# An adaLN transformer block on one core: the work re-cut into items whose issue order on every engine is fixed in the kernel, with four MLP chunks of 512 tokens

## The chip, the cores and the metric

The kernel runs on one core of one Trainium2 chip. The time is device microseconds of one execution, and lower is better. All inputs and the output are bf16 in device memory (HBM). The page of the profile calls the engines PE (TensorE, matmuls; PEld is its weight load), DVE (VectorE), ACT (ScalarE), POOL (GpSimd) and SP (SyncE, which here only starts DMAs).

## What is computed

2048 tokens of width 448 pass through two halves of a block. Each half is modulated by vectors made from a condition `c`. Cut to what matters:

```python
mod = silu(c) @ w_mod                      # six vectors sa, ca, ga, sb, cb, gb of 448
h = layernorm(x) * (1 + ca) + sa
q, k, v = h @ wqkv                         # 16 heads of 28
# position s sees s, s-2, s-4, ... s-14 (window 8, dilation 2; masked below 0)
x = x + ga * (softmax(q k^T * 28**-0.5 over the 8) v) @ wo
h = layernorm(x) * (1 + cb) + sb
y = layernorm(h)
x = x + gb * (gelu(y @ w1 + b1) @ w2 + b2) # 448 -> 1792 -> 448
```

Even and odd positions never see each other, so the kernel loads the even tokens as blocks 0 to 7 and the odd ones as blocks 8 to 15, and the dilated window becomes 8 neighbouring columns.

## The kernel before, in words

**Start.** SP loads `c`, the first four token blocks and the weights needed first; eleven dummy matmuls (`idle_ps`, L144) run meanwhile. `ps_col` (L236) gives the columns `ca` and `sa`. The weights of q and k are copied into a layout padded to 32 per head (`Wqk`, L249 to L254).

**Front end**, once for each four blocks (512 tokens): statistics and normalise on DVE (`ln_params`, L163, with a power on POOL at L173; `normalize`, L176), 16 transposes on PE into `ptr` (L194), four DVE passes that scale and shift into `hT` (L198), then eight `pq` groups of four 512-column matmuls (L206). ACT moves the four q tiles out of PSUM (L210), DVE the four k tiles (L212).

**Attention**, 17 blocks `g` of 121 queries against 128 keys (`attention_block`, L323): `pv` (L330, moved out by ACT), the logits `lt` in two halves of eight 28-row matmuls each (L341; each half alternates between two of the four 32-row strips of the array), exp on ACT (L347), a multiply by a banded mask on DVE (L351), `po` (16 small matmuls, L363), a division on DVE (L365, L367), four transposes `pt` (L371), moved into `oT` by ACT (L377). `wo_block` (L381) multiplies by `wo` (already scaled by `ga`) and DVE adds the residual (L387) into a tile of its own, `x1_all`.

**MLP**, 8 steps `j` of 256 tokens: `mlp_front` (L391) runs two layer norms in a row for each block on DVE (L395 on POOL prepares the residual plus bias), a DMA transpose into `yT` (L407), then 14 weight tiles in groups of four: `p1` (L418, 256 columns a matmul) and one gelu a group (L422, 1024 columns). `mlp_back` (L446) multiplies by `w2` (L451), and `mlp_finish` (L437) adds the residual on DVE (L440) and stores four blocks at a time. The last step runs its second matmul fused into the first (`w2_partial`, L431 and L434).

**Order.** Exp and gelu need different tables on ACT, and a switch is an ACT_TABLE_LOAD. So the kernel runs five phases (L456): some attention blocks, then one or two MLP steps, and `order_after` (L58) adds scheduling edges that keep the exps of a phase together and the gelus together. `mlp_back` of a phase is put among the attention blocks of the next. Within these edges the tile framework's scheduler interleaves the instructions of each engine. PSUM has eight banks: `ps_lt` two tiles of two banks (shared by `ptr`, `lt`, `p1`), `ps_a` two (`po`, `pt`, `pw`), `ps_b` two (`pq`, `pv`, the modulation rows, `p2`). `w2_scale_piece` (L313) multiplies `w2` by `gb` in 14 pieces in the first phase.

Of the kernel before, what the change touches and what calls it, by code (L numbers as in the profile page):

```python
# [14 lines left out]
DP = 512  # L15
# [13 lines left out]
NIDLE = 11  # L29
SCHED = mybir.DependencyInfo(mybir.DependencyClass.NoSync, mybir.DependencyReason.SCHED_ONLY)  # L30
SYNC = mybir.DependencyInfo(mybir.DependencyClass.Sync, mybir.DependencyReason.SCHED_ONLY)


@with_exitstack
def kernel(
# [31 lines left out]

    bulk_dmas = []
# [8 lines left out]
    ps_a = ctx.enter_context(tc.tile_pool(name="ps_a", bufs=2, space=bass.MemoryType.PSUM))  # L77
    ps_b = ctx.enter_context(tc.tile_pool(name="ps_b", bufs=2, space=bass.MemoryType.PSUM))

    def ps_att(shape, dtype, name):  # L80
        return ps_a.tile(shape, dtype, name=name, tag="a1")

    def ps_small(shape, dtype, name):
        return ps_b.tile(shape, dtype, name=name, tag="b1")
# [5 lines left out]
    x1_all = cst.tile([128, NBLK, D], BF16, name="x1_all")  # L90
    x_all = cst.tile([128, NBLK, D], BF16, name="x_all")
    NX1P = 6
# [3 lines left out]
    def x1_blk(b):  # L96
        return x1_all[:, b, :]
# [10 lines left out]
    ident = cst.tile([128, 128], BF16, name="ident")  # L108
    mask_rest = cst.tile([128, H, BK], BF16, name="mask_rest")
# [8 lines left out]
    wk = ctx.enter_context(tc.tile_pool(name="wk", bufs=3))  # L118
# [3 lines left out]
    stp = stp_cm.__enter__()  # L122
    c_row = stp.tile([1, D], BF16, name="c_row")
    nc.sync.dma_start(out=c_row[:], in_=c)
    xv = xs.rearrange("s (jb p) d -> p s jb d", p=128)
    nc.sync.dma_start(out=x_all[:, 0:4, :], in_=xv[:, 0, 0:4, :])
# [6 lines left out]
    bulk_dmas.append(nc.sync.dma_start(out=x_all[:, 4:8, :], in_=xv[:, 0, 4:8, :]))  # L133

    for zb in zbufs:
        nc.vector.memset(zb[:, D:DP], 0.0)
# [5 lines left out]
    for i in range(NIDLE):  # L142
        idle_ps = ps_att([128, 512], FP32, "idle_ps")
        nc.tensor.matmul(idle_ps[:], lhsT=idle_in[:, 0:128], rhs=idle_in[:], start=True, stop=True)  # L144
# [6 lines left out]
    nc.gpsimd.memset(wmod[64:128, KT - 1, :], 0.0)  # L151
    nc.gpsimd.memset(Wv[64:128, KT - 1, :], 0.0)
    nc.gpsimd.memset(Wqk[64:128, KT - 1, :, :], 0.0)
    for kt in range(KT):
        kr = 128 if kt < KT - 1 else 64
        nc.gpsimd.memset(Wqk[0:kr, kt, :, :].rearrange("p m (r e) -> p m r e", e=32)[:, :, :, DH:32], 0.0)
    pad_ranges = [(0, PADF), (PADF + S, WT)]
# [4 lines left out]

    def ln_params(srcs, nm):  # L163
        n = len(srcs)
        mv = sm.tile([128, n, 2], FP32, name=f"mv_{nm}", tag=f"mv{n}")
        for i, src in enumerate(srcs):
            st = sm.tile([128, 6], FP32, name=f"st_{nm}", tag="st")
            nc.vector.bn_stats(out=st[:], in_=src)  # L168
            nc.vector.bn_aggr(out=mv[:, i, :], in_=st[:])
        tv = sm.tile([128, n], FP32, name=f"tv_{nm}", tag=f"tv{n}")  # L170
        nc.vector.tensor_scalar_add(out=tv[:], in0=mv[:, :, 1], scalar1=EPS)  # L171
        rs = sm.tile([128, n], FP32, name=f"rs_{nm}", tag=f"rs{n}")
        nc.gpsimd.tensor_tensor(out=rs[:], in0=tv[:], in1=neg_half[:, 0:n], op=ALU.pow)  # L173
        return mv, rs

    def normalize(dst, src, mv, rs, i):  # L176
        nc.vector.tensor_scalar(out=dst, in0=src, scalar1=mv[:, i, 0:1], scalar2=rs[:, i:i + 1],  # L177
                                op0=ALU.subtract, op1=ALU.mult)

    zcount = [0]  # L180
# [3 lines left out]

    def front_end_ln(c4):
        bs4 = [c4 * 4 + i for i in range(4)]
        mv, rs = ln_params([x_all[:, b, :] for b in bs4], "ln1")
        ptr = ps_lt.tile([128, KT, 512], BF16, name="ptr", tag="lt")
        for i in range(4):
            z = zbufs[zcount[0] % NZB]  # L190
            zcount[0] += 1
            normalize(z[:, 0:D], x_all[:, bs4[i], :], mv, rs, i)
            for kt in range(KT):
                nc.tensor.transpose(out=ptr[:, kt, i * 128:(i + 1) * 128], in_=z[:, kt * 128:(kt + 1) * 128],  # L194
                                    identity=ident[:])
        c0 = tok_col(bs4[0])
        for kt in range(KT):
            nc.vector.tensor_scalar(out=hT[:, kt, c0:c0 + 512], in0=ptr[:, kt, :], scalar1=ca1_col[:, kt:kt + 1],  # L198
                                    scalar2=sa_col[:, kt:kt + 1], op0=ALU.mult, op1=ALU.add)

    def front_end_qk(c4):
        cc0 = tok_col(c4 * 4)
        for m in range(8):
            pq = ps_small([128, 512], FP32, "pq")
            for kt in range(KT):
                nc.tensor.matmul(pq[:], lhsT=Wqk[:, kt, m, :], rhs=hT[:, kt, cc0:cc0 + 512],  # L206
                                 start=(kt == 0), stop=(kt == KT - 1))
            dst = (qT if m < 4 else kT)[:, m % 4, cc0:cc0 + 512]
            if m < 4:
                nc.scalar.copy(out=dst, in_=pq[:])  # L210
            else:
                nc.vector.tensor_copy(out=dst, in_=pq[:])  # L212
# [14 lines left out]
    silu_bf = stp.tile([128, KT], BF16, name="silu_bf")  # L227
    nc.vector.tensor_tensor(out=silu_bf[:], in0=e_c[:], in1=c_col[:], op=ALU.mult)
    nc.vector.tensor_copy(out=silu_bc[:], in_=silu_bf[:].unsqueeze(2).to_broadcast([128, KT, 128]))

    ps_col = ps_small([128, 2 * KT], FP32, "ps_col")
    for v in range(2):
        for j in range(KT):
            nj = 128 if j < KT - 1 else 64
            for kt in range(KT):
                nc.tensor.matmul(ps_col[0:nj, v * KT + j:v * KT + j + 1],  # L236
                                 lhsT=wmod[:, kt, v * D + j * 128:v * D + j * 128 + nj],
                                 rhs=silu_bf[:, kt:kt + 1], start=(kt == 0), stop=(kt == KT - 1))
# [7 lines left out]
    nc.vector.tensor_copy(out=sa_col[0:64, KT - 1:KT], in_=ps_col[0:64, KT - 1:KT])  # L246
    for kt in range(KT):
        kr = 128 if kt < KT - 1 else 64
        wq_out = Wqk[0:kr, kt, :, :].rearrange("p m (r e) -> p m r e", e=32)[:, :, :, 0:DH]  # L249
        wq_in = wqk_st[0:kr, kt, :].rearrange("p (m r d) -> p m r d", m=8, r=4)  # L250
        if kt in (0, 2):
            nc.vector.tensor_copy(out=wq_out, in_=wq_in)
        else:
            nc.scalar.copy(out=wq_out, in_=wq_in)  # L254

    front_end_ln(0)
    front_end_qk(0)

    stp_cm.__exit__(None, None, None)
    stp_cm = tc.tile_pool(name="setup2", bufs=1)  # L260
    stp = stp_cm.__enter__()
    wmod2 = stp.tile([128, KT, 4 * D], BF16, name="wmod2")
    nc.gpsimd.memset(wmod2[64:128, KT - 1, :], 0.0)
    bulk_dmas += load_ktiles(nc.sync, wmod2, w_mod[:, 2 * D:6 * D], 0)
    nc.gpsimd.memset(wo_s[0:ZR_N, KT - 1, :], 0.0)
    bulk_dmas += load_ktiles(nc.sync, wo_s, A_wo, ZR_N)
    bulk_dmas.append(nc.sync.dma_start(out=x_all[:, 8:NBLK, :], in_=xv[:, 1, :, :]))
    mk0 = nc.gpsimd.memset(mask_rest[:], 1.0)
    wait_for([mk0], wv_loads[1:], "mask building (GpSimd) after the DVE-critical start")
    nc.gpsimd.affine_select(out=mask_rest[:], in_=mask_rest[:], pattern=[[0, H], [1, BK]], compare_op=ALU.is_ge,  # L270
                            fill=0.0, base=WIN - 1, channel_multiplier=-1)
    nc.gpsimd.affine_select(out=mask_rest[:], in_=mask_rest[:], pattern=[[0, H], [-1, BK]], compare_op=ALU.is_ge,
                            fill=0.0, base=0, channel_multiplier=1)
# [5 lines left out]

    def mod_bc(idx, name):  # L280
        pb = ps_small([128, D], FP32, name)
        for kt in range(KT):
            nc.tensor.matmul(pb[:], lhsT=silu_bc[:, kt, :], rhs=wmod2[:, kt, (idx - 2) * D:(idx - 1) * D],
                             start=(kt == 0), stop=(kt == KT - 1))
        return pb

    pb_ga = mod_bc(2, "pb_ga")
    nc.vector.tensor_tensor(out=wo_s[:, 0:KT - 1, :], in0=wo_s[:, 0:KT - 1, :],
                            in1=pb_ga[:, :].unsqueeze(1).to_broadcast([128, KT - 1, D]), op=ALU.mult)
    nc.vector.tensor_tensor(out=wo_s[ZR_N:128, KT - 1, :], in0=wo_s[ZR_N:128, KT - 1, :], in1=pb_ga[ZR_N:128, :],  # L290
                            op=ALU.mult)
# [4 lines left out]
    b2_bc = stp.tile([128, D], BF16, name="b2_bc")  # L296
    bulk_dmas.append(nc.sync.dma_start(out=b2_bc[:], in_=B_b2.partition_broadcast(128)))
    wait_for(bulk_dmas, wv_loads[1:], "bulk loads after the critical loads")
    order_after(bulk_dmas[1:], bulk_dmas[:1], "bulk loads in need-order")
    pb_sb = mod_bc(3, "pb_sb")  # L300
    nc.scalar.copy(out=sb_bc[:], in_=pb_sb[:])
    pb_cb = mod_bc(4, "pb_cb")
    nc.vector.tensor_scalar_add(out=g2_bc[:], in0=pb_cb[:], scalar1=1.0)
# [9 lines left out]
    def w2_scale_piece(n):  # L313
        for _ in range(n):
            if not w2_scale_todo:
                return
# [217 lines left out]
```

## Time and profile before

| what | value |
|---|---|
| median of 3 runs | 227.32 us (226.48 to 229.45) |
| the profiled execution | 226.5 us, span of the core 224.4 us |
| instructions in the span | 4134 |
| busy: PE, PE weight load | 196.3 us (87%), 118.0 us (53%) |
| busy: DVE, ACT, POOL | 149.2 us (66%), 103.1 us (46%), 54.9 us (24%) |
| mean granted PE clock | 0.973 |
| first `pq` matmul starts | 14.52 us |
| first `p1` matmul starts | 77.20 us |
| last PE work ends | about 219.6 us |

The span runs from the first to the last recorded instruction; the execution's time is 2.1 us more. "Busy" of PE is the union of the matmuls' records, each of which lasts from its start until its last column has left the array, so neighbours overlap: a 448-column matmul has a record of 353 ns, while a dense row of them starts one every 0.19 us. To price PE work one therefore takes start to start. The same holds for DVE and ACT to a smaller degree.

### The profile page before, as it was taken

To read this page: it belongs to the slowest core of one execution; us is meant where nothing else is said; L and a number is where in the kernel's file an instruction comes from. 1 tells how busy PE (TensorE), PEld (TensorE's weight loads), DVE (VectorE), ACT (ScalarE), POOL (GpSimd) and SP (SyncE) were. 2 spreads that over 40 slices of the span, in tenths; PEclk is the share of its full clock that TensorE was granted. 3 is DMA by queue.
4 is the path that set the end of the run, shared out by engine and by line. 5 is a ranking of instruction groups with operands and counts; after the bars stand their busy time and mean duration, and the time that the engine had idled before them with its cause. 6 is when DMAs were issued, how large, how long until landed. Compare 5 with 4: busy or idle time off the path is not lost.

```text
span 224.4 us, 4134 instructions
## 1 busy us (share of the span) xinstructions
PE 196.3 (87%) x1671; PEld 118.0 (53%) x1671; DVE 149.2 (66%) x367; ACT 103.1 (46%) x133; POOL 54.9 (24%) x89
## 2 busy tenths in 40 slices
PE   7479985999789899979699988796999899989992
PEld 2343352545364485447585444475854476575760
DVE  2786999999888962587865586858755862561102
ACT  2304376143713068497448316763483257352320
POOL 7399001102214220115340023023213230020000
PEclk9999999999958999999999999889999999999998
DMA  5799960000001111001102201100122011021002
GB/s 186 253 325 319 339 218 0 3 0 0 3 0 23 26 26 25 3 0 26 23 0 50 82 0 26 23 3 1 23 50 82 0 26 23 3 82 23 3 0 82
DMA packets 17766, 13.37 MB, mean 60 GB/s; under 512 B 9042, under 2 KB 16851, under 8 KB 17748
## 3 DMA queue, kind: packets, MB, share of 16 engines
q1 hardware_dynamic: 17748, 13.12, 19.6%
q8 instruction: 13, 0.21, 0.4%
q14 instruction: 5, 0.04, 0.1%
HBM read 9.18 MB, written 1.84 MB: 49 GB/s over the span
## 4 chain that ended last, share of the span: by engine, by line
PE 60%; DVE 21%; ACT 10%; POOL 5%; issue 2%; DVEq 0%; POOLq 0%; ACTq 0%
PE p L418 16%; PE p L451 14%; PE pq L206 9%; PE pw L385 5%; ACT hm L422 4%; DVE et L351 3%; POOL rs_ln L173 3%; PE po L363 3%; DVE st_ln L168 3%; DVE x_all L387 3%; DVE kT L212 2%; PE p L434 2%; PE idle_ps L144 2%; PE pt L371 2%; POOL x1p_ring L395 2%
## 5 line engine op out<-in xcount | busy, mean ns | idle before, releaser
L418 PE MATMUL p<-yT,w_s 128*128 128x256 bf16 x448 | 54.5, 277 | 1.5 <-ACT hm L422 0.7
L418 PEld LDWEIGHTS <-w_s 128*128 128x128 bf16 x448 | 43.6, 99 | 10.1 <-issue 2.9
L173 POOL TENSOR_TENSOR rs_ln<-tv_ln,neg_half 128x1 f32<-128x1 f32 (+1 forms) x36 | 22.5, 628 | 79.8 <-DVE tv_ln L171 76.1
L422 ACT ACTIVATE hm<-p 128x1024 bf16<-128x1024 f32 (+1 forms) x32 | 28.6, 916 | 28.7 <-PE p L418 28.5
L451 PE MATMUL p<-w_s,hm 128*128 128x448 bf16 x196 | 40.1, 353 | 0.0
L347 ACT ACTIVATE et<-lt 128x1024 bf16<-128x1024 f32 x34 | 33.6, 1031 | 8.7 <-PE lt L341 8.6
L206 PE MATMUL pq<-hT,Wqk 128*128 128x512 bf16 x128 | 33.6, 401 | 4.4 <-ACT qT L210 2.7
L395 POOL TENSOR_TENSOR x1p_ring<-x_all,gbb_bc 128x448 f32<-128x448 bf16 x16 | 17.8, 1113 | 65.6 <-DVE x_all L387 60.3
L440 DVE TENSOR_TENSOR x_all<-p,x1p_ring 128x448 bf16<-128x448 f32 x16 | 9.8, 619 | 26.9 <-PE p L451 16.5
L377 ACT COPY oT<-pt 128x484 bf16<-128x484 bf16 (+3 forms) x18 | 9.7, 542 | 36.3 <-PE pt L371 36.3
L451 PEld LDWEIGHTS <-hm 128*128 128x128 bf16 x196 | 18.1, 97 | 15.6
L206 PEld LDWEIGHTS <-Wqk 128*128 128x128 bf16 x128 | 12.7, 102 | 19.7 <-issue 9.2
L168 DVE BATCH_NORM_STATS2 st_ln<-x_all 128x6 f32<-128x448 bf16 x32 | 19.1, 609 | 3.5 <-DMA x_all<-in_A_x_dram 3.3
L351 DVE TENSOR_TENSOR et<-et,mask_rest 128x2048 bf16<-128x2048 bf16 x17 | 20.6, 1209 | 0.0
L330 PE MATMUL pv<-Wv,hT 128*128 128x448 bf16 x68 | 17.2, 354 | 0.2 <-DVE kT L212 0.2
L387 DVE TENSOR_TENSOR x_all<-pw,x_all 128x448 bf16<-128x448 f32 x16 | 9.9, 621 | 10.2 <-PE pw L385 10.2
L385 PE MATMUL pw<-wo_s,oT 128*128 128x448 bf16 x64 | 15.7, 370 | 1.1 <-ACT oT L377 0.9
L210 ACT CAST qT<-pq 128x512 bf16<-128x512 f32 x16 | 9.1, 587 | 14.0 <-PE pq L206 14.0
L341 PE MATMUL lt<-qT,kT 28*128 28x128 bf16 x272 | 13.6, 217 | 1.8 <-ACT et L347 0.8
L341 PEld LDWEIGHTS <-kT 28*128 28x128 bf16 x272 | 8.1, 93 | 12.2 <-issue 11.5
L177 DVE TENSOR_SCALAR ybuf<-h,mv_ln,rs_ln 128x448 bf16<-128x448 bf16 x16 | 7.7, 483 | 9.1 <-POOL rs_ln L173 9.0
L177 DVE TENSOR_SCALAR z<-x_all,mv_ln,rs_ln 128x448 bf16<-128x448 bf16 x16 | 6.3, 395 | 10.2 <-POOL rs_ln L173 10.1
(87 smaller groups left out, 207.7 us busy)
## 6 DMA issues: line engine op xcount, KB each, us to landing
out_dram<-x_all SPq DMA_DIRECT2D x4, 448.0 KB, 2.7
w_s<-in_B_w_dram SPq DMA_DIRECT2D x1, 1568.0 KB, 11.4
wmod<-in_w_mod_dram SPq DMA_DIRECT2D x1, 1344.0 KB, 7.1
w_s<-in_B_w_dram SPq DMA_DIRECT2D x1, 1344.0 KB, 13.9
x_all<-in_A_x_dram SPq DMA_DIRECT2D x2, 448.0 KB, 3.6
x_all<-in_A_x_dram SPq DMA_DIRECT2D x1, 896.0 KB, 9.5
wmod<-in_w_mod_dram SPq DMA_DIRECT2D x1, 672.0 KB, 5.0
wqk_st<-in_A_wqkv_dram SPq DMA_DIRECT2D x1, 672.0 KB, 6.0
```

The lines of the kernel that those rows point to most:

```text
L168: nc.vector.bn_stats(out=st[:], in_=src)
L173: nc.gpsimd.tensor_tensor(out=rs[:], in0=tv[:], in1=neg_half[:, 0:n], op=ALU.pow)
L206: nc.tensor.matmul(pq[:], lhsT=Wqk[:, kt, m, :], rhs=hT[:, kt, cc0:cc0 + 512], start=(kt == 0), stop=(kt == KT - 1))
L330: nc.tensor.matmul(pv[:], lhsT=hT[:, kt, k0:k0 + BK], rhs=Wv[:, kt, :], start=(kt == 0), stop=(kt == KT - 1))
L341: mm = nc.tensor.matmul(lt[:, rr, ft * BK:(ft + 1) * BK], lhsT=kT[32 * r:32 * r + DH, ft, k0:k0 + BK], rhs=qT[32 * r:32 * r + DH, ft, q0:q ...
L347: ex = nc.scalar.activation(out=et_v[:, 2 * half:2 * half + 2], in_=lt[:].rearrange("p r (ft c) -> p r ft c", ft=4), func=ACT.Exp, scale=f ...
L351: nc.vector.tensor_tensor(out=et[:], in0=et[:], in1=mask_rest[:], op=ALU.mult)
L385: nc.tensor.matmul(pw[:], lhsT=oT[:, kt, jb * 128:(jb + 1) * 128], rhs=wo_s[:, kt, :], start=(kt == 0), stop=(kt == KT - 1))
L395: nc.gpsimd.tensor_tensor(out=x1p_ring[:, b % NX1P, :], in0=x1_blk(b), in1=gbb2_bc[:], op=ALU.add)
L418: mm = nc.tensor.matmul(p1[:, f, :], lhsT=w1_s[:, kt, ft * 128:(ft + 1) * 128], rhs=yT[:, kt, :], start=(kt == 0), stop=(kt == KT - 1))
L422: g = nc.scalar.activation(out=hm[:, fq:fq + nf, :], in_=p1[:, 0:nf, :], func=ACT.Gelu_apprx_tanh)
L451: nc.tensor.matmul(p2[:], lhsT=hm[:, ft, bi * 128:(bi + 1) * 128], rhs=w2_s[:, ft, :], start=(ft == 0), stop=(ft == FT - 1))
```

## The change

Nothing of the arithmetic on the tokens changes. What changes is how the work is cut, which engine takes it, and who orders it.

- A class `Plan` takes every piece of work after the loads as an item: its engine or engines with a price in us, the items that it needs, and the buffers that it takes and uses. `order()` gives each item the length of the longest chain behind it, lays the items out one after another by earliest start (ties by longest chain), and picks ACT or DVE for an item that both can do. The items are emitted by their start in that layout, under `manual_schedule()`: each engine issues in that order, and the framework adds only the semaphores.
- The eviction of q and k tiles, the scale and shift into `hT`, the eviction of `pv` and the copy into `oT` may each go to ACT or DVE. In the built program DVE is left with 7 of the 40 q and k evictions, 11 of 20 `hT` passes and 3 of 17 `pv` evictions, and gets 10 of the 17 `oT` copies.
- The MLP works on four chunks of 512 tokens (`CH`): `p1` holds two weight tiles of 512 columns, so 224 matmuls of 512 columns stand for 448 of 256. The gelus stay at 1024 columns, 28 of them.
- Attention blocks per phase (`PHASES`): 10, then 3, 3 and 1. In the built program ACT loads a table 12 times in all, against 10: of each of the first three chunks, gelus 0 and 6 are issued first, then exps of an attention block, then gelus 1 to 5.
- The logits of a block are one item of 16 matmuls that steps through all four row strips in turn.
- PSUM: three banks for all small tiles (tag `s`) and one for `p2`; `p2` of the last chunk's last three blocks uses `s`.
- The two layer norms of the MLP run for two blocks at a time; `w2` is scaled in three pieces during the first MLP chunk; `x1` is written over `x`; each block is stored alone (16 stores for 4).
- Start: the first four blocks come in two loads and go through two front ends of 256 tokens. The mask is built small on POOL and copied wide by DVE. All setup stands in the program ahead of the items, so on DVE the first token statistics follow the columns `ca` and `sa`, two `Wqk` copies, `silu_bc` and the mask copy. The dummy matmuls are 4, 6 and 3, around the condition's matmuls.

```diff
+CH = [(0, 4), (4, 8), (8, 12), (12, 16)]
+PHASES = [10, 13, 16, 17]
+W2S = [(0, 5), (5, 10), (10, 14)]
+SLOTS = {"lt": 2, "s": 3, "p2": 1, "et": 2, "on": 2, "vb": 3, "z2": 2, "yT": 2, "hm": 2, "xp": 4}
+class Plan:
+    def order(self, hop=0.07, table=1.3):
...
+        for i in reversed(out):
+            o = ops[i]
+            tail[i] = min(o["eng"].values()) + o["lag"] + o["pri"] + max([tail[k] + hop for k in succ[i]], default=0.0)
...
+                fin = {e: max(t, free[e]) + d for e, d in o["eng"].items()}
+                e = min(fin, key=lambda e: (fin[e], e))
+                s = max(t, free[e])
+                if o["tab"] and tab not in (None, o["tab"]):
+                    s += table
+                key = (s, -tail[i], i)
+                if best is None or key < best[0]:
+                    best = (key, i, e, s)
...
+    ctx.enter_context(tc.manual_schedule())
-    ps_a = ctx.enter_context(tc.tile_pool(name="ps_a", bufs=2, space=bass.MemoryType.PSUM))
-    ps_b = ctx.enter_context(tc.tile_pool(name="ps_b", bufs=2, space=bass.MemoryType.PSUM))
+    ps_s = ctx.enter_context(tc.tile_pool(name="ps_s", bufs=SLOTS["s"], space=bass.MemoryType.PSUM))
+    ps_p2 = ctx.enter_context(tc.tile_pool(name="ps_p2", bufs=SLOTS["p2"], space=bass.MemoryType.PSUM))
...
+            P.add(f"qe{b0}.{m}", {"ACT": 0.06 + w / 1164, "DVE": 0.07 + w / 960}, needs=[f"qk{b0}.{m}"],
+                  uses=[f"pq{b0}.{m}"], fn=e_fn)
...
+            for ft in range(4):
+                for r in range(4):
+                    nc.tensor.matmul(lts[r // 2][:, r % 2, ft * BK:(ft + 1) * BK],
...
+        for q in range(FT // 2):
+            P.buf(f"p1{c}.{q}", "lt")
+            def fn(e, q=q):
+                p1 = T["p1", c, q] = ps_lt.tile([128, 2, 512], FP32, name="p1", tag="lt")
...
+            P.add(f"w1{c}.{q}", {"PE": 8 * w / 2400}, needs=[f"yt{b}" for b in bs] + ["w1"], uses=[f"yT{c}"],
+                  after=w1_after, allocs=[f"p1{c}.{q}"], lag=0.17, fn=fn)
...
+            P.buf(f"p2{b}", "s" if last and bi >= SLOTS["p2"] else "p2")
...
+            P.add(f"fin{b}", {"DVE": 0.54}, needs=[f"w2{b}.{FT // 2 - 1}", f"xp{b}"], uses=[f"p2{b}", f"xp{b}"],
+                  fn=f_fn)
...
+    for c, upto in enumerate(PHASES):
+        for g in range(g0, upto):
+            attention(g, last_ge, last_w1 + ([f"lt{g - 1}"] if g else []))
+            last_ex = [f"ex{g}.1"]
+        g0 = upto
+        mlp_items(c, last_ex, [f"lt{g0 - 1}"])
+        last_w1 = [f"w1{c}.{FT // 2 - 1}"]
+        last_ge = [f"ge{c}.{FT // 2 - 1}"]
+    todo = P.order()
+    for i in todo:
+        o = P.ops[i]
+        if o["fn"]:
+            o["fn"](o["ran"])
```

Item names used below: `qk4.0` is the first q tile of the front end that begins at block 4; `lt`, `ex`, `mk`, `po`, `on`, `pt`, `ot` with a number are the steps of that attention block; `wo` and `x1` of that token block; `w1 c.q`, `ge c.q` the group q (two weight tiles) of chunk c and its gelu; `w2 b.q` the second matmul of block b for that group (two matmuls); `fin b` the eviction of `p2` with the residual.

## The prediction

> **What bounds the kernel now.** I read the page first, then the table of stages, then the timelines of PE, DVE and ACT.
>
> ```profile
> PE 196.3 (87%) x1671; PEld 118.0 (53%) x1671; DVE 149.2 (66%) x367; ACT 103.1 (46%) x133; POOL 54.9 (24%) x89
> PE   7479985999789899979699988796999899989992
> DVE  2786999999888962587865586858755862561102
> ```
>
> PE looks 87% busy and full nearly everywhere. But a record lasts until the matmul has drained, so gaps shorter than a drain count as busy. The timeline of PE gives the true prices, start to start:
>
> ```profile
> 84.57 0.89 PE L341 MATMUL lt<-qT,kT 28*128 28x128 bf16 x16
> 85.39 4.71 PE L451 MATMUL p<-w_s,hm 128*128 128x448 bf16 x24
> 90.07 0.57 PE L363 MATMUL po<-vbuf,et 128*128 128x29 bf16 x16
> 90.48 0.92 PE L451 MATMUL p<-w_s,hm 128*128 128x448 bf16 x4
> 91.65 0.40 PE L371 MATMUL pt<-ident,on 128*128 128x128 bf16 x4
> 91.88 0.54 PE L330 MATMUL pv<-Wv,hT 128*128 128x448 bf16 x2
> 112.72 6.28 PE L418 MATMUL p<-yT,w_s 128*128 128x256 bf16 x56
> 118.83 0.35 PE L451 MATMUL p<-w_s,hm 128*128 128x448 bf16 x1
> ```
>
> Sixteen `lt` take 85.39 - 84.57 = 0.82 us, sixteen `po` 0.41, four transposes 0.23, a 448-column matmul 4.68 / 24 = 0.19, a 256-column one 6.11 / 56 = 0.109. A 512-column `pq` costs 0.217 (eight from 51.67 to 53.40).
>
> PE work of the whole kernel by these: `p1` 448 x 0.109 = 48.9; `p2` 224 x 0.19 = 42.6; `pq` 128 x 0.217 = 27.8; `pv`, `pw` and modulation 148 x 0.19 = 28.1; `lt` 17 x 0.6 = 10.2 (the trace has sets of 0.82 and others near 0.36; I take the middle); `po` 7.0; `pt` and `ptr` 7.6. Together 172. Between the first `pq` (14.5) and the last `p2` (219.6) lie 205 us. So PE is fed only 84% of that time: 33 us are waits. Where:
>
> ```profile
> 24.00:77.00 53.00, 46.16 (x375) 23.38 (x373) 47.81 (x116) 22.51 (x34) 9.27 (x11) 0.94 0.18 53
> 77.00:121.00 44.00, 40.07 (x400) 27.38 (x400) 30.07 (x76) 27.78 (x35) 10.94 (x15) 1.00 0.09 17
> 121.00:165.00 44.00, 39.19 (x385) 25.07 (x383) 31.23 (x74) 23.52 (x30) 9.22 (x14) 0.96 0.11 27
> 204.00:219.60 15.60, 15.60 (x108) 10.35 (x106) 1.25 (x2) 3.67 (x4) 0.00 (x0) 1.00 0.05 9
> ```
>
> Columns: stage, length, then busy of PE, PE weight load, DVE, ACT, POOL, granted PE clock. In 24 to 77 DVE is busy 47.8 of 53 us and ACT 22.5: DVE is the bound there. What PE does in it is, by the prices, 5 blocks of attention, 96 `pq`, four `pw`, the modulation: about 40 us. So 13 us are lost, and some 18 in 77 to 204, where exps, masks and the norms of the next MLP step hand over one after another. At the end PE is the bound.
>
> **The change part by part.**
>
> *PE work* stays: 448 matmuls of 256 columns become 224 of 512; 28 groups x 8 x 0.217 = 48.6 against 48.9. For `lt` the order changes from two strips to four. Bounds: 0.82 a block as above, and 0.41, the `po` row, which loads as many weights. I keep 0.6; the ends are 17 x 0.2 = 3.5 us either way. A rule on this: the Trainium skill, "TensorE: Matmul & The Clock Gate" (Part 3), has matmuls on four different row strips run together, 3.07 times as fast at 512 columns. By it a block would take about 0.3 us, an estimate from that page, and the total be some 5 us lower; two strips in turn gave 51 ns a matmul here, about one after another, so I hold to the rows.
>
> *DVE in the front ends.* Sixteen k evictions leave (0.61 each start to start, 9.8 us), 3 half and 4 full ones come back (3.5); nine of 20 `hT` passes leave (about 3 us); `w2` scaling (14 x 0.31 = 4.3) moves behind the first gelus; 3 `pv` evictions and the mask copy come (2.2). ACT takes over and had 30 us free. DVE's first 77 us become some 11 us lighter: that removes the bound of this stretch.
>
> *Start.* DVE issues in order, and the token statistics now stand behind the columns and copies:
>
> ```profile
> 9.68 0.16 DVE L243 TENSOR_SCALAR ca_col<-ps_col 128x3 f32<-128x3 f32 x1 [1.10 <-PE ps_col L236]
> 9.96 0.68 DVE L252 COPY Wqk<-wqk_st 128x896 bf16<-128x896 bf16 x2
> 10.56 2.66 DVE L177 TENSOR_SCALAR zbuf<-x_all,mv_ln,rs_ln 128x448 bf16<-128x448 bf16 x4
> 14.52 3.40 PE L206 MATMUL pq<-hT,Wqk 128*128 128x512 bf16 x8 [0.64 <-DVE hT L198]
> ```
>
> Before, the four statistics were done by 7.9, beside the weight load. After: columns done about 9.7 (limited by the same load), `Wqk` 10.4, `silu_bc` 10.8 (0.46 here), mask 11.5 (four times as long a copy: between 0.6 and 1.3), three statistics at 0.6 to 13.4, POOL's power to 14.2 (0.58 to 1.03), normalise, transpose and `hT` of two blocks: first `pq` at 16.3, 1.8 later. The SP queue: x in two loads sets the weights back by 0.45 us at most (one issue).
>
> *Waits for single buffers.* With one `p2` bank, the next block's `w2` waits for the eviction: drain 0.16 + eviction 0.62 + hand-over 0.05 = 0.8. The built order has such neighbours without other work between at blocks 0-1, 3-4, 6-7, 7-8, 8-9, 10-11, 11-12: 7 x 0.8 = 5.6 us. Below nothing it can't go; if DVE is busy with a mask (1.14) when the block ends, 2 us each.
>
> *Table loads:* two more.
>
> ```profile
> 84.89 0.54 ACT L332 CAST vbuf<-pv 128x448 bf16<-128x448 f32 x1
> 85.45 1.28 ACT L347 ACT_TABLE_LOAD   x1
> 86.75 1.94 ACT L347 ACTIVATE et<-lt 128x1024 bf16<-128x1024 f32 x2
> ```
>
> A switch costs 1.3 us, from the end of one instruction to the next, so 2.6 us of ACT, which is 46% busy. It also stands before a matmul's buffer is free. The skill's page "ScalarE: Activation LUTs" (What ACT_TABLE_LOAD costs) adds a drain of 1.38 us to the load, 2.66 a switch, and (Table sets) asks to finish one set before the next, which speaks against this order; no drain shows in this row. By the page eleven switches would cost 15 us more of ACT, and the sum perhaps 5 more.
>
> *MLP chains.* A chunk's first matmul waits for four transposed blocks, not two. In the built order each chunk's norms lie beside the `w2` of the chunk before (12 us of PE between `wo15` and the last chunk), so I cost it at nothing; if that cover fails, the chain of the last pair is residual 0.54, statistics 0.6, power 0.6, normalise 0.64, scale and shift 1.2, statistics 1.2, power 0.6, normalise 0.64, two transposes 1.2 + 2.4 (issue, median landing): 9.6 us. Queues: on POOL a residual of 1.11 can stand ahead of a power; on SP twelve more stores (0.38 an issue) stand ahead of transposes, up to three in a row, each behind its `fin`. DVE issues those `fin` before the normalise that the transpose needs, so nothing is added for either.
>
> *Sum.* By stage of the built order, PE and DVE work at the prices above (DVE: mask 1.14, statistics 0.60, normalise 0.32, division 0.70, evictions 0.54, all start to start):
>
> - first `pq` to `qk4.0`: PE 13.7, DVE 12.1. Add 1.7 because the first eight `pq` start cold (3.40 us for eight here against 1.73) and 1.5 for hand-overs: 16.9.
> - to `w1 0.0`: PE 44.2, DVE 41.6. Nearly even, so each waits for the other: the next stage, followed by hand, lost 9%; I add 8%: 48.
> - to `w1 1.0`: PE 27.6, DVE 28.0. Item by item: `wo8` waits 0.65 for the eviction of `wo7`, `w1 0.1` 0.85 for the exp behind a table load, `w2 1.0` 0.8 for `p2`: 30.0.
> - to `w1 2.0`: PE 28.5, DVE 15.6: 29.4 the same way.
> - to `w1 3.0`: PE 28.0, DVE 18.4, three `p2` waits 2.4 and 0.6: 31.0.
> - to the end of `p2`: PE 30.0, two waits 1.6 and 0.1: 31.7.
> - tail: drain and eviction 0.8, store 3.6 as now (220.8 to 224.4; a smaller store could save up to 1): 4.4.
>
> 16.3 + 16.9 + 48 + 30.0 + 29.4 + 31.0 + 31.7 + 4.4 = 207.7 us of span, with the 2.1 around it 209.8. That is against the profiled execution's 226.5; the median of the runs is 0.4% above it, which gives 210.5.
>
> **The rivals.**
>
> *Tighter* (under 205). The four strips pack (-3.5) and the even stretch loses 2% instead of 8 (-4): about 202. For it: ACT has room. Against it: three `s` banks for all small tiles in strict turn, where there were four.
>
> *The same losses as before* (217 to 232). If fixed order feeds PE no better than 84%, 172 / 0.84 = 205 from 16.3 on, + 4.4 + 2.1 = 228: no change. For it: in-order engines cannot step past a late item, and one ring of three banks ties `pq`, `pv`, `po`, `pt` and `pw` together. Against it: the DVE bound of 24 to 77 is really lighter. The half-way case is 219.
>
> *Slower* (over 232). Each `fin` stands in DVE's fixed order behind norms and masks. If at each of 15 block changes PE waits for it not 0.8 but 0.8 + 1.45 more, 21.8 us are added and it passes 232; that takes more than a mask (1.14) ahead at every change. Against it: DVE is 15 to 18 us busy in the 30 us stages where nine of them fall, and nearly idle (3.8 of 30) where six do.
>
> *It does not do what it says.* Exps and gelus are not kept in four phases, as the built order shows (eleven switches); this is costed above, and there is no more to lose.
>
> **How the numbers follow.** Chances: as summed (205 to 217) 0.55; tighter 0.10; half-way (217 to 222.8) 0.12; same losses (222.8 to 231.9) 0.14; slower 0.09. The likeliest gives 210.5. The range leaves out 0.07 below 203 and 0.13 above 226. Two per cent of 227.3 is 4.5 us, about what a measurement of this kernel can tell from no change: faster 0.55 + 0.10 + 0.12 = 0.77, within it 0.14, slower 0.09.
>
> **What would show it.** First `pq` near 16.3; `w1 0.0` near 81 with ten attention blocks behind it; DVE busy not over 90% in any long stage; waits of `p2` on `fin` near 0.8 us, seven of them; eleven switches; the last chunk's `p1` directly behind `w2`; `lt` of 16 between 0.4 and 0.8. I am wrong if `w1 0.0` comes after 90, or if PE waits for DVE in the last 100 us by more than 10 us.

## The result and the profile after

The changed kernel takes 218.62 us (median of 4 runs, 217.38 to 219.07); the kernel before, run beside it, 226.9 (226.04 to 229.45). The ratio is 0.9636, 95% interval 0.9585 to 0.9686: 8.3 us faster. The forecast of 210.5 was 16 to 17 us faster, so the direction and the range held and half of the gain did not come. The profiled execution took 217.38 us, its span is 215.7. Some executions of a kernel run at a lower clock and take over 1.5% longer than its fastest one: medians and ranges here hold them, ratios and intervals do not (of the ten with four strips in the kernel before, seven were like that, hence 230.95 beside a ratio of 1.0044).

From the page of the changed kernel, busy time by engine and then the 40 slices (5.4 us each):

```profile
PE 186.4 (86%) x1466; PEld 96.4 (45%) x1481; DVE 142.9 (66%) x327; ACT 111.8 (52%) x142; POOL 45.2 (21%) x72
PE   7247994999999789988596999998999888999973
DVE  2076697979999887899998868626788671000232
PEclk9755997699999999999979999999999999999999
```

PE is busy 9.9 us less than before and idle 1.2 us more (29.3 against 28.1): the share of busy time says nothing of the gain. Counted from 0, slices 1 to 3, 6 and 7, and 20 have a low granted clock (half speed in part or all of the slice; such matmuls are called cold below); the stages that came out longer than forecast lie beside them. Start to start, against the sum:

| stage | forecast | measured |
|---|---|---|
| to the first `pq` | 16.3 | 19.3 |
| to `qk4.0` | 16.9 | 17.8 |
| to `w1 0.0` | 48 | 49.1 |
| to `w1 1.0` | 30.0 | 34.6 |
| to `w1 2.0` | 29.4 | 28.9 |
| to `w1 3.0` | 31.0 | 30.8 |
| to the end of `p2` | 31.7 | 31.6 |
| tail | 4.4 | 3.6 |

Most of the 8.0 us of span that are missing lies in two stages: the start (3.0) and the first MLP chunk (4.6). The last three long stages are right within 0.5 us each. Against the kernel before, the first `pq` comes 4.8 us later and the way from there to the end of `p2` is 12.3 us shorter (192.8 against 205.1): the gain lies behind the start. The table of stretches (same columns as in the prediction; the first three are cut near the borders of stages, the last is the fourth stage itself) shows where DVE is full:

```profile
33.00:81.00 48.00, 42.08 (x417) 21.50 (x417) 43.81 (x99) 31.95 (x48) 5.83 (x6) 0.93 0.08 21
81.00:111.00 30.00, 26.35 (x215) 13.15 (x217) 27.30 (x58) 18.61 (x22) 8.22 (x8) 0.94 0.07 14
111.00:140.00 29.00, 27.06 (x224) 13.81 (x226) 22.89 (x51) 18.69 (x19) 8.33 (x8) 1.00 0.13 32
86.21:120.77 34.56, 29.27 (x227) 14.20 (x229) 31.81 (x67) 20.62 (x24) 12.80 (x11) 0.95 0.09 20
```

DVE is busy 91% in 33 to 81 and again in 81 to 111, then 79%; in the fourth stage 92%. PE's waits, longest first (us in total, times, longest):

```profile
PE p L686 <- DVE x_all L693: 6.2, 7, 1.7
PE ptr L430 <- DVE zbuf L400: 4.2, 1, 4.2
PE ps_col L326 <- DMA wmod<-in_w_mod_dram: 3.9, 2, 3.6
PE lt L522 <- DVE hT L441: 2.6, 2, 1.5
PE pt L584 <- DVE on L577: 2.2, 2, 2.0
```

The first row is the seven waits of `w2` for `fin` (forecast: seven, 5.6 us). The second and third lie one behind the other at the start.

### The profile page after: what moved, and what is told of

Same layout as the page of the kernel before. It is cut to its first block, busy times and chain, and to the rows that moved or that the text cites. A ratio compares the mean times of both kernels' runs of the same rounds, so it can differ in the third digit from the quotient of the medians.

```text
span 215.7 us, 3681 instructions
## 1 busy us (share of the span) xinstructions
PE 186.4 (86%) x1466; PEld 96.4 (45%) x1481; DVE 142.9 (66%) x327; ACT 111.8 (52%) x142; POOL 45.2 (21%) x72
## 4 chain that ended last, share of the span: by engine, by line
PE 55%; DVE 31%; POOL 4%; DMA 3%; ACT 2%; issue 2%; SPq 1%; POOLq 0%
PE p L686 16%; PE pq L452 13%; PE p L660 12%; DVE st L385 6%; POOL rs L395 4%; PE pv L557 4%; PE pw L605 4%; DVE z L629 3%; DMA wmod<-in_w_mod_dram 3%; DVE x_all L693 3%; DVE z L400 2%; DVE et L542 2%; DVE on L577 2%; DVE mv L386 2%; DVE x_all L610 2%
## 5 line engine op out<-in xcount | busy, mean ns | idle before, releaser
L660 PE MATMUL p<-yT,w_s 128*128 128x512 bf16 x213 | 52.0, 385 | 1.6 <-ACT et L533 0.9
L667 ACT ACTIVATE hm<-p 128x1024 bf16<-128x1024 f32 x28 | 28.6, 1023 | 35.9 <-PE p L660 35.7
L395 POOL TENSOR_TENSOR rs<-tv,neg_half 128x2 f32<-128x2 f32 (+1 forms) x21 | 19.3, 923 | 111.3 <-DVE tv L392 111.3
L452 PE MATMUL pq<-hT,Wqk 128*128 128x512 bf16 (+1 forms) x156 | 33.0, 360 | 3.1 <-DVE wo_s L485 1.7
L660 PEld LDWEIGHTS <-w_s 128*128 128x128 bf16 x224 | 21.8, 99 | 25.9 <-issue 2.4
L452 PEld LDWEIGHTS <-Wqk 128*128 128x128 bf16 x160 | 15.9, 104 | 16.9 <-issue 5.0
L385 DVE BATCH_NORM_STATS2 st<-x_all 128x6 f32<-128x448 bf16 x32 | 19.6, 612 | 0.2
L378 ACT CAST kT<-pq 128x512 bf16<-128x512 f32 (+1 forms) x18 | 9.3, 517 | 4.4 <-PE pq L452 4.0
L577 DVE TENSOR_TENSOR on<-po,rden 128x448 bf16<-128x448 f32 x17 | 10.6, 625 | 0.6
L378 ACT CAST vbuf<-pv 128x448 bf16<-128x448 f32 x14 | 7.4, 536 | 6.8 <-PE pv L557 6.7
L385 DVE BATCH_NORM_STATS2 st<-z 128x6 f32<-128x448 bf16 x16 | 9.8, 611 | 0.1
```

The lines of the kernel that those rows point to most:

```text
L378: nc.scalar.copy(out=out, in_=in_)
L385: nc.vector.bn_stats(out=st[:], in_=src())
L395: nc.gpsimd.tensor_tensor(out=rs[:], in0=T["tv", tile_key][:], in1=neg_half[:, 0:n], op=ALU.pow)
L452: nc.tensor.matmul(pq[:, 0:w], lhsT=Wqk[:, kt, m, :], rhs=hT[:, kt, c0:c0 + w], start=(kt == 0), stop=(kt == KT - 1))
L660: nc.tensor.matmul(p1[:, f, 0:w], lhsT=w1_s[:, kt, ft * 128:(ft + 1) * 128], rhs=T["yT", c][:, kt, 0:w], start=(kt == 0), stop=(kt == KT - 1))
L667: nc.scalar.activation(out=T["hm", c][:, 2 * q:2 * q + 2, 0:w], in_=T["p1", c, q][:, :, 0:w], func=ACT.Gelu_apprx_tanh)
```

## The experiments

Times are medians of 4 executions of the same kernel unless another count stands there, ratios are against the kernel before on the same chip. The changed kernel without more edits stands at 218.62 and 0.9636.

### The start

**One load of x.**

```diff
-    nc.sync.dma_start(out=x_all[:, 0:2, :], in_=xv[:, 0, 0:2, :])
-    nc.sync.dma_start(out=x_all[:, 2:4, :], in_=xv[:, 0, 2:4, :])
+    nc.sync.dma_start(out=x_all[:, 0:4, :], in_=xv[:, 0, 0:4, :])
```

> The first four blocks of x come in one load again instead of two. Theory (the late start is due to the second load that stands ahead of the weights): the modulation weights land 1 to 1.5 us earlier, the first pq at 17.5 to 18.3 instead of 19.3 us, total 216 to 217.5. Rival (the transfers fill the same queues however they are cut, or the statistics wait for the larger load instead): first pq 19 to 20 us, total 218 to 219.

Measured 215.93 us (214.85 to 216.52), ratio 0.9504 (0.9433 to 0.9575). The modulation weights land 4.9 us after issue instead of 6.8, the first `pq` is at 16.68, and the 2.5 us last to the end of `p2`. The theory held, with more than it asked for.

**Statistics ahead of the modulation evictions.** The statistics and roots of the first four blocks are written ahead of `ca_col`; their items in the layout stay, but emit nothing.

> The statistics and reciprocal roots of the first four blocks are emitted ahead of the evictions of the modulation products, so that DVE does them while it waits for the modulation weights. Theory (the chain modulation products, mask copy, statistics, normalisation is in series at the start): first pq 2 to 3.5 us earlier, at 16 to 17.3 instead of 19.3 us, total 215 to 217. Rival (the first pq waits for its weights, or the gain is given back in the stage up to w1 0.0): first pq 19 us or total 217.5 to 219.

Measured 213.5 us (213.26 to 214.24), ratio 0.9408 (0.9362 to 0.9454): first `pq` at 16.03. Here are DVE in the changed kernel, where it stands idle 7.16 us for the modulation product and does the statistics after it,

```profile
11.97 0.16 DVE L334 TENSOR_SCALAR ca_col<-ps_col 128x3 f32<-128x3 f32 x1 [7.16 <-PE ps_col L326]
13.18 0.68 DVE L501 COPY mask_rest<-mask 128x2048 bf16<-128x2048 bf16 x1
13.79 0.61 DVE L385 BATCH_NORM_STATS2 st<-x_all 128x6 f32<-128x448 bf16 x1
17.02 0.70 DVE L400 TENSOR_SCALAR zbuf<-x_all,mv,rs 128x448 bf16<-128x448 bf16 x2
```

and DVE with the statistics ahead, where the product comes no earlier (12.10) but the normalisation (`zbuf`) follows directly on the copies:

```profile
12.10 0.16 DVE L345 TENSOR_SCALAR ca_col<-ps_col 128x3 f32<-128x3 f32 x1 [3.92 <-PE ps_col L337]
13.31 0.68 DVE L511 COPY mask_rest<-mask 128x2048 bf16<-128x2048 bf16 x1
13.91 1.49 DVE L410 TENSOR_SCALAR zbuf<-x_all,mv,rs 128x448 bf16<-128x448 bf16 x4
```

So the late start has two links of about 3 us each: weights that land late, and statistics that DVE, issuing in order, could only begin after them. The total fell by more (5.1) than the 3.3 us at the first `pq`; 4.1 of it can be seen in the profiled executions.

**Both.**

> One load of the first four blocks of x and the statistics ahead of the modulation evictions, together. Theory (two separate links of the starting chain: the weights land later, and DVE begins the statistics only after them): first pq at 13 to 14.5 instead of 19.3 us, total 210 to 212. Rival (both mend the same 3 us): first pq 16 us, total 213 to 214.5.

Measured 213.37 us (212.65 to 213.72), ratio 0.9354 (0.9316 to 0.9392). The first `pq` is at 14.63, 1.4 us earlier than with the statistics alone, but `qk4.0` is at 33.59 against 33.65. So the rival held for the total (213 to 214.5), though not for its first `pq` of 16. PE with both edits, and then with the statistics alone:

```profile
14.63 7.00 PE L461 MATMUL pq<-hT,Wqk 128*128 128x256 bf16 x40
21.57 0.40 PE L531 MATMUL lt<-qT,kT 28*128 28x128 bf16 x16
```

```profile
16.03 5.65 PE L462 MATMUL pq<-hT,Wqk 128*128 128x256 bf16 x40
21.62 0.40 PE L532 MATMUL lt<-qT,kT 28*128 28x128 bf16 x16
```

The same 40 matmuls take 6.94 us from an earlier start and 5.59 from a later one. With both edits the granted clock is 0.50 from 14.63 to 19.20 and 1.00 after it (0.67 over the 40). With the statistics alone the profile has no record of the clock before 17.8 us and shows 1.00 there, but the starts tell: the 16 transposes ahead (14.35 to 16.03) begin every 0.105 us, where four on a full clock take 0.23, so that clock too was at half, and full from about 17.7. So the earlier start met a clock that rose 1.5 us later; on a cold clock it gained nothing. (The kernel before has no record ahead of 17.6 us either, so its mean of 0.973 counts its start as full.)

### The first MLP chunk

**No xp.** An `xp` is the sum of a block's residual and its scaled bias, made on POOL for the block's `fin`. In the changed kernel POOL does four of them in a row, because the modulation row `pb_gb` that they need comes only then.

```diff
-                  after=[f"xp{b - 1}"] if b else [], fn=x_fn)
+                  after=[f"xp{b - 1}"] if b else [], fn=None)
...
-                nc.vector.tensor_tensor(out=x_all[:, b, :], in0=T["p2", b][:], in1=x1p_ring[:, b % NX1P, :],
+                nc.vector.tensor_tensor(out=x_all[:, b, :], in0=T["p2", b][:], in1=x1_blk(b),
```

> The changed kernel with POOL's residual-plus-bias items xp left out and its layout kept; the last addition takes the residual x1 straight from its tile, so the bias row that the modulation scales is left out of the output. Port theory (DVE operations slow down while POOL streams xp): with layout and all other work the same, the second normalisation at 0.70 instead of 2.15 us, ybuf at 0.40 instead of 1.11, ml at 0.6 instead of 1.45, stage w1 0.0 to w1 1.0 at 30 to 31.5 instead of 34.6 us, total 213.5 to 215.5. Rival (the operations are long for another reason, or the stage is bound by the late modulation row and not by POOL): they stay long, total 217.5 to 219.

Measured 215.94 us (214.32 to 216.53), ratio 0.946 (0.9407 to 0.9512), 2.7 us below the changed kernel (1.8 between the profiled executions). The last addition itself takes 0.62 us either way. POOL in the changed kernel,

```profile
99.78 5.04 POOL L677 TENSOR_TENSOR x1p_ring<-x_all,gbb_bc 128x448 f32<-128x448 bf16 x4 [0.43 <-DVE gbb_bc L490]
```

DVE in it beside that,

```profile
99.62 1.22 DVE L542 TENSOR_TENSOR et<-et,mask_rest 128x2048 bf16<-128x2048 bf16 x1
100.75 2.15 DVE L400 TENSOR_SCALAR z<-x_all,mv,rs 128x448 bf16<-128x448 bf16 x2
102.82 1.11 DVE L400 TENSOR_SCALAR ybuf<-z,mv,rs 128x448 bf16<-128x448 bf16 x1
103.85 1.45 DVE L629 TENSOR_TENSOR z<-z,g_bc 128x896 bf16<-128x896 bf16 x1
```

and the same four groups without `xp`:

```profile
99.84 1.22 DVE L542 TENSOR_TENSOR et<-et,mask_rest 128x2048 bf16<-128x2048 bf16 x1
100.97 0.70 DVE L400 TENSOR_SCALAR z<-x_all,mv,rs 128x448 bf16<-128x448 bf16 x2
101.58 0.39 DVE L400 TENSOR_SCALAR ybuf<-z,mv,rs 128x448 bf16<-128x448 bf16 x1
101.89 0.62 DVE L629 TENSOR_TENSOR z<-z,g_bc 128x896 bf16<-128x896 bf16 x1
```

Same work, same order: 2.15 to 0.70, 1.11 to 0.39, 1.45 to 0.62, three us of DVE. Only the mask, which began 0.16 us before POOL did, keeps its 1.22; the POOL operation that began behind it took 1.96, the longest of the 16 `xp` (median 1.05). The Trainium skill, "SBUF — State Buffer" (SBUF: two separate sides), says that GpSimd and certain DVE operations (two SBUF inputs, or a two-port mode) share one pair of ports which is held for a whole instruction, so that the later one stands still; these rows agree.

The stage fell only to 33.0 us, short of the 30 to 31.5 expected. PE is 3.6 us ahead at the last `w1` group of the chunk (107.36 against 110.97), and then loses 2.3: it waits longer for the first `fin`, and its matmuls after that run slowly. PE without `xp`, and in the changed kernel:

```profile
114.46 3.52 PE L686 MATMUL p<-w_s,hm 128*128 128x448 bf16 x10 [2.23 <-DVE x_all L693]
```

```profile
109.36 1.40 PE L605 MATMUL pw<-wo_s,oT 128*128 128x448 bf16 x4
117.27 2.05 PE L686 MATMUL p<-w_s,hm 128*128 128x448 bf16 x10 [1.69 <-DVE x_all L693]
```

Ten matmuls take 3.52 us after a wait of 2.23 and 2.05 after one of 1.69. In the changed kernel it was the `pt` at 106.19, late by 1.96 behind DVE's slow operations, that was followed by cold matmuls (clock 0.50 in 107.6 to 109.4, four `pw` in 1.40 instead of 0.92). In these two places a wait of 2 us is paid nearly twice. But the length of the wait does not decide it. With both start edits the `pt` waits the same 1.96 and the clock stays at 1.00, and behind the same wait of 2.23 the ten matmuls take 2.05:

```profile
112.56 2.05 PE L695 MATMUL p<-w_s,hm 128*128 128x448 bf16 x10 [2.23 <-DVE x_all L702]
```

What decides it stays open.

**The modulation row forward.** The item `pb_gb` gets a priority of 70 in the layout, which is planned anew.

> The item of the modulation row pb_gb, on which all the residual-plus-bias items xp wait, gets a priority that draws it forward; the layout is planned anew around it, so the xp items are spread over the chunk-0 stage and no longer stand four in a row on POOL. Port theory (DVE operations on two SBUF operands slow down while POOL streams from SBUF: the normalisation 2.15 against 0.70 us, ybuf 1.11 against 0.40, ml 1.45 against 0.62): no operation of DVE above 1.2 us in that stage, w1 0.0 to w1 1.0 falls from 34.6 to 30 or 31 us, total 213.5 to 215.5. Rival (DVE is simply full in that stage, POOL has nothing to do with it): the stage stays at 34 to 35 us, total 218 to 219.

Measured 214.43 us (214.1 to 217.62), ratio 0.9438 (0.9361 to 0.9515). The stage is 29.8 us, with two `z` in 0.70 and `ml` (the product with `g_bc`) at 0.62, as the theory says. The price is not gone everywhere: in the stage before, where `xp` now fall, two `z` take 1.40 at 60.64 and 1.41 at 74.81. But the row's evictions and the `w2` scalings, 4.9 us of DVE, have only moved: `w1 0.0` comes 5.0 us later, and `w1 1.0` at 121.02 against 120.77. These stages are those of an execution of 217.62; where the other three, of 214.1 to 214.6, are shorter stays open.

**All together**, with the edit of the next heading.

> One load of x, statistics ahead, each PSUM bank of a transposed block read by one engine, and the modulation row pb_gb drawn forward; the layout is planned anew for the last of these. Theory (the start and the xp items cost what was found one by one, 5 to 7 and 4 us, and lie in different stages): total 204.5 to 208. Rival (the stages in between take the time back): 209 to 213.

Measured 212.21 us (211.08 to 213.2), ratio 0.9306 (0.925 to 0.9362): the best version here, 6.4 us below the changed kernel, but nearer to the rival. Against the two start edits alone (213.37) little is left: `w1 0.0` is at 86.77 against 81.56, `w1 1.0` at 116.51 against 116.06. With the start edits alone DVE is busy 92% of both stages; here it is 94% of the longer and 85% of the shorter one, and 6.8 us of the longer one (70.4 to 77.2) run at a clock of 0.50. So work moved into a stage that was as full, which fits a bound on DVE; what the cold stretch took was not tested apart.

### One engine to a PSUM bank

```diff
+                e = "ACT" if kt < 2 else "DVE"
```

> The four copies of a transposed block (hT) are no longer dealt in turn to ACT and DVE; the two tiles of one PSUM bank go to ACT, the two of the other to DVE. Nothing else moves. Theory (the two engines wait for each other because they read the same bank): the waits of ACT for DVE's hT (8.1 us in 6 in the profiled execution) and of DVE for ACT's (3.1 us in 6) go, the way to qk4.0 gets 1 to 3 us shorter, total 215 to 217.5. Rival (they wait for TensorE's transposes and only the record names the other engine): hT as before, total 218 to 219.

Measured 217.1 us (216.71 to 217.94), ratio 0.957 (0.9488 to 0.9653). ACT's waits for DVE's `hT` (8.1 us before the edit) are gone, with one of 4.9 for PE's transposes in their place, but DVE still waits for ACT's (3.0 us in 5), and `qk4.0` is at 37.53 against 37.14. The way there is not shorter: the theory held for one of the two waits and fell for the time, and 1.5 us of median with overlapping intervals prove nothing.

### The logits

**Two strips again.** In the changed kernel:

```diff
-            for ft in range(4):
-                for r in range(4):
+            for ft, r in [(f, 2 * hf + rr) for hf in range(2) for f in range(4) for rr in range(2)]:
+                if True:
```

> The changed kernel with the old order of the logit matmuls: eight through two strips, then eight through the other two. Layout and all else stay. If the packing of four strips is what shortened lt (0.34 us for 16 in the profiled execution against 0.82 before): lt back at 0.8 us; with every block's TensorE time on the path, plus 16 x 0.48 = 7.7 us, total 224 to 227; if the difference is hidden by waits in part: plus 2 to 5 us. Rival (lt is short for another reason, such as fewer semaphore waits): no change, 218 to 219.

Measured 218.55 us (217.95 to 219.27), ratio 0.963 (0.9572 to 0.9689): no change at all. PE with four strips, and with two:

```profile
46.56 0.41 PE L522 MATMUL lt<-qT,kT 28*128 28x128 bf16 x16
46.90 0.36 PE L557 MATMUL pv<-Wv,hT 128*128 128x448 bf16 x1
```

```profile
84.74 0.43 PE L522 MATMUL lt<-qT,kT 28*128 28x128 bf16 x16
85.10 0.57 PE L567 MATMUL po<-vbuf,et 128*128 128x29 bf16 x16
```

Sixteen take 0.34 us one way and 0.36 the other. The order of the strips is not what made them short.

**Four strips in the kernel before.** Both tiles of a block are taken first, then all 16 are issued in the order of the change.

> The kernel before, with one part of the change alone: the 16 logit matmuls of a block issued one after another through all four row strips, instead of two groups of eight through two strips. Theory 1 (the packing is worth its time wherever it stands): 16 blocks at 0.82 to 0.34 us, minus 4 to 8 us, total 219 to 223. Theory 2 (TensorE is starved by other engines in this kernel, so that a shorter logit group only waits longer): minus 0 to 2 us, total 225 to 227.5; it may lose, since the first half's exponential now waits for both halves' tiles to be free.

Measured 230.95 us over 10 executions (227.1 to 233.13), ratio 1.0044 (0.9973 to 1.0115): no gain. Groups of instructions, kernel before and this one (busy us, mean ns):

```profile
L341 PE MATMUL lt<-qT,kT 28*128 28x128 bf16 x272 | 13.6, 217 | 1.8 <-ACT et L347 0.8
```

```profile
L339 PE MATMUL lt<-qT,kT 28*128 28x128 bf16 x272 | 12.9, 218 | 1.0 <-ACT et L347 0.2
```

In the changed kernel the group has 7.6 us, with two strips 8.0. The 6 us between are not all PE work: in the kernel before, the scheduler cuts the 17 sets into 33 pieces with other matmuls between, and each piece ends with a record of 0.22 us that overlaps what follows. Five sets stand uncut with a stop of 0.3 us after the eighth matmul, four of them where gelu gives way to exp; these are the sets of about 0.82 that the prediction read. PE, and then ACT beside it, in the kernel before:

```profile
84.57 0.40 PE L341 MATMUL lt<-qT,kT 28*128 28x128 bf16 x8
85.06 0.40 PE L341 MATMUL lt<-qT,kT 28*128 28x128 bf16 x8
```

```profile
83.50 1.51 ACT L422 ACTIVATE hm<-p 128x1024 bf16<-128x1024 f32 x2 [1.08 <-PE p L418]
```

The ninth matmul starts 0.05 us after ACT's last gelu has ended (85.01). The logits take their two tiles from the same ring as `p1`, so the second half waits for the tile that this gelu still reads. The edit does not reach that: at 85.59 the chip again runs eight matmuls, stops until a gelu ends (86.03) and runs eight more from 86.08, although the program lists them strip by strip.

### The order

**The scheduler free.** `tc.manual_schedule()` is left out of the changed kernel.

> The changed kernel without the fixed issue order: the framework's own scheduler may move instructions on each engine. Theory (the order written by the layout is what brings the gain): TensorE waits come back, total 222 to 232. Rival (the gain is that of four chunks of 512 tokens and of the packing, the scheduler would keep or better the order): 215 to 219.

Measured 218.45 us (217.58 to 221.33), ratio 0.9608 (0.9552 to 0.9664): the rival held. The scheduler draws the statistics forward by itself (first `pq` at 16.33) and gives the 3 us back later: PE's waits for `fin` are 8.6 us instead of 6.2, and the longest, of 3.5 instead of 1.7, has ten cold matmuls behind it (3.43 us instead of 2.05).

**No rule in the layout.**

```diff
-                key = (s, -tail[i], i)
+                key = (s, i)
```

> The layout without its rule: among items that could start at the same moment the one defined first goes first, not the one with the longest remaining chain. Theory (the rule carries the gain): TensorE waits for blocks whose chain was begun late, total 224 to 245. Rival (the earliest possible start decides nearly always, the rule only settles ties): 216 to 222.

Measured 272.93 us (272.75 to 273.99), ratio 1.1968 (1.1916 to 1.202). The theory held in its direction; the size lies far beyond its 245. One row of PE's waits has 40.8 of the 54 us:

```profile
PE p L660 <- DMA yT<-ybuf: 40.8, 3, 14.6
```

Three of four chunks begin after the whole chain from the last residual to the transposed block, with PE idle for 14 us and its mean clock at 0.85.

**p2 in a ring of four banks**, shared with the other short products.

> The product p2 takes its PSUM tile from a common ring of four banks with the other short-lived products, instead of one bank of its own; the layout is planned anew. Theory (the seven waits of p2 for fin, 6.2 us together, are due to the one bank): they fall under 2 us, total 213.5 to 216. Rival (the ring makes the logit and projection products wait instead, or DVE's turn moves the wait elsewhere): 217 to 221.

Measured 226.06 us over 10 executions (224.16 to 226.5), ratio 0.9938 (0.99 to 0.9975). The waits for `fin` fell from 6.2 to nothing, as the theory said, and the new layout lost more elsewhere: PE's waits for `zbuf` are 10.3 us instead of 4.2, and one of 13.5 is new. PE before the last chunk:

```profile
181.27 0.93 PE L605 MATMUL pw<-wo_s,oT 128*128 128x448 bf16 x4
195.69 0.59 PE L660 MATMUL p<-yT,w_s 128*128 128x512 bf16 x1 [13.49 <-DMA yT<-ybuf]
```

It is the same uncovered chain, once. So the run does not tell what the one bank costs by itself.

## Why the prediction was right and wrong

**Start: wrong by 3.0.** The step "x in two loads sets the weights back by 0.45 us at most (one issue)" failed: an issue's time is no bound on what a split load does to the transfers behind it. The weights landed 1.9 us later (6.8 against 4.9 with one load). The modulation product stood at 11.97 instead of 9.7, which is 2.3 of the 3.0; with one load it stands at 9.37. The prediction's "limited by the same load" was a misreading as well: in the kernel before, the product waited for DVE's `silu_bf` and not for the load,

```profile
8.14 1.50 PE L236 MATMUL ps_col<-silu_bf,wmod 128*128 128x1 bf16 x32 [1.46 <-DVE silu_bf L228]
```

and its 32 matmuls took 1.50 us. In the changed kernel 29 of them take 2.39, and with one load 2.19 though most of these run at a clock of 1.00 (7.14 to 8.90): the cold clock is not the main reason. Every fourth now works on 64 rows instead of 128, a part of the change that the prediction did not price; whether that is the reason was not tested. The rest of the 3.0 is the chain behind it, 5.5 us from the first statistics to the first `pq` instead of 4.8; a block's statistics cost 0.73 with their second step, not 0.60.

**First chunk: wrong by 4.6.** The step "on POOL a residual of 1.11 can stand ahead of a power" looked at POOL's queue alone and added nothing. The price was on DVE: four `xp` in a row stretched three of its groups by 3.0 us. The run without `xp` shows that; 2.7 us of total hang on them. The rest of the excess seems to lie with DVE, busy 31.8 of the stage's 34.6 us (29.6 of 33.0 without `xp`), and with PE's waits of about 2 us and the slow matmuls after some of them; it was not split further. For those slow matmuls the sum had 1.7 us, at the first eight `pq` only. At `qk4.0` alone they cost 2 us: 30 `pq` from 37.96 to 46.56 are 0.287 each, where the version with all edits takes 0.222.

**`lt`: mis-sized, in the other direction.** 0.34 a set lies below the lower bound of 0.41. The "51 ns a matmul" through two strips was read off a set with a stop in its middle; without the stop two strips take 0.36 for 16, 22 ns each. 17 x 0.26 = 4.4 us of PE work are gone that the sum still held. They do not show as a gain: ten of the 17 sets lie before `w1 0.0`, in stages that came out 2 us longer than summed. That these two stages stand so near the sum is luck in part: 2.6 us less for `lt` against the 2 us of cold matmuls at `qk4.0` and a DVE that is fuller than summed (44.4 us against 41.6). The rule of the Trainium skill that the prediction set aside ("TensorE: Matmul & The Clock Gate", Part 3) gave 0.3 and was nearer, but the run with two strips shows that the strips are not its cause here.

**`p2`: right.** Seven waits of 6.2 us for seven of 5.6; the one of 1.7 is the first, behind the late stage.

**Table loads: right.** Eleven in the groups of exp and gelu below, 1.28 each and 0.1 us of idle time before them, so no drain shows:

```profile
L667 ACT ACT_TABLE_LOAD x6 | 7.7, 1283 | 0.1
L533 ACT ACT_TABLE_LOAD x5 | 6.4, 1283 | 0.1
```

**MLP chains covered at no cost: right in this layout**, and now with a price. The prediction put an uncovered chain at 9.6 us; PE waits 13.5 to 14.6 for one.

**DVE lighter in the front ends: right in direction only.** DVE's busy time in all fell from 149.2 to 142.9 us and ACT's rose from 103.1 to 111.8. But DVE is still 91% busy in 33 to 81, against the prediction's own sign of "not over 90%".

**The rivals.** The half-way case (217 to 222.8) is what came, but not for its reason: the losses were not spread as 84% of everywhere, they sat at two places, and three stages ran as summed. In the tighter rival the "-4" is too much: 2% instead of 8% of the even stretch's 44.2 us is 2.7.

**Where the gain came from** stays open in the main. The fixed issue order is worth nothing over the scheduler (218.45), the four strips nothing (218.55), and where the order is fixed the rule of the layout is needed (272.93 without). What is left of the change (four chunks of 512 tokens, evictions that ACT or DVE can take, the new division of PSUM, norms for two blocks at a time) was not tested part by part. Of the fall of `lt` from 13.6 to 7.6 us much is overlap, as said above, so it does not answer the question.

## What to carry to other kernels

When work moves on one engine, look at what runs at that moment on the engine that shares its ports, and price its instructions there, not only its queue. In a kernel whose engines issue in order, whatever can be done while the first weights are under way has to be issued ahead of their first user. A mended wait is worth its length only if the next thing, such as a full DVE or a cold PE clock, does not take it: of two cures of 3 us at the start, the second gained nothing.

## What the runs showed of the hardware

- Splitting one 448 KB load into two of 224 KB set the loads queued behind it back by 1.9 us (6.8 against 4.9 us from issue to landing; 6.7 against 5.1 in the pair with the statistics ahead), four times the issue's own 0.45.
- The granted clock did not go by the length of a wait. A wait of 1.96 us was followed by a clock of 0.50 in the changed kernel and stayed at 1.00 with both start edits; behind a wait of 2.23 us ten matmuls took 3.52 us without `xp` and 2.05 with both start edits. A start 1.4 us earlier met a clock that became full 1.5 us later (19.2 against about 17.7).
- A DVE operation that began 0.16 us before POOL kept its time (1.22); those that began beside a running POOL operation took two to three times theirs, and the POOL operation that began behind the running DVE one took 1.96 instead of 1.05.
